# Transforms along c and back on 64x64 tiles of the array, small products on 32-column tiles, output strips queued as one step, and a new explicit order

## The chip, the cores and the metric

The kernel runs on one core of a Trainium2 chip. The metric is the device time of one execution in microseconds (us); lower is better. Five engines work side by side: PE (TensorE, matrix products and transposes, with PEld for its weight loads), DVE (VectorE), ACT (ScalarE), POOL (GpSimd) and SP, which here issues every transfer between HBM and on-chip memory. Each engine executes its own instructions in order and waits at a semaphore where it needs another engine's result.

## The reference

```python
X = np.fft.fft(x, axis=1)                 # x: 8 x 2496 x 256, f32
X = np.fft.fft(X, axis=2)
x = X.real.reshape(19968, 256)
logits = x @ phi                          # 32 slots = 8 experts x 4
d = softmax(logits, over the 19968 tokens)
slot_input = d.T @ x
for e in range(8):                        # 4 slots for each expert
    slot_out[e] = relu(slot_input[e] @ w1[e]) @ w2[e]      # 256 -> 1024 -> 256
c = softmax(logits, over the 32 slots)
return c @ slot_out                       # 19968 x 256, f32
```

The real part of the transform is never formed. The transform over the features is folded into phi, and the one over the sequence (2496 = 64 x 39) is made on the logits: first along a (64 values), then along c (39 values, of which 20 are kept by symmetry). The softmax weights over the tokens go back the same way and are multiplied with x itself.

## The kernel before

The eight batches are four pairs p = 0 to 3. The whole program is a list of steps, PLAN, written out by hand: each step calls one small function, and the order of the list is the order of the instructions on every engine. A step is a kind with its numbers, after a slash the engine of its copy (a for ACT, v for DVE, g for GpSimd), and after an equals sign the buffers in which its tiles live: `A000/a=et000:E1`. The buffers ("homes") are R (6 of 8 KB a partition: x tiles, w1, output tiles), E (18 of 4 KB: folded x, w2, turned weights), M and D (logits and exponentials), X (spread maxima) and B (the 8 banks of PSUM). A step that takes a home waits until all users of its last occupant are done; a transfer that waits for a home holds up everything behind it in SP's queue.

The kinds, in the order in which one pair goes through them:

- X, XT, C, P, I, J: loads of x (5 tiles a pair, 1024 or 896 KB), of pair 3's x once more turned over, constants, phi, w1 (8 of 1024 KB) and w2 (16 of 512 KB).
- F (or FT), G, H: folds of x on DVE, L292, L298, L303. T, A: transposes on PE (L308) and their copy. Zo, Ze, Zt, Y: products with the phi tables on 128x32 tiles (L323, L341) and copy. t, y: transpose (L362) and copy into the layout of the next step.
- a, b: transform along a (L381): for each group of three slots one product of 128 moving columns with 120 output rows. l, m: transform along c (L398), cosine and sine part, each one product of 120x120 with up to 384 moving columns. L, M, N: copy, sum and difference.
- R, V, v, vb, W, w: the maxima. E: exponentials on ACT, L448. q: sum and difference on DVE, L453.
- e, f: transform back along c (L460): for each group four products with 32 output rows, side by side on 32-column tiles, 120 moving columns each. d, D: back along a (L476). u, U: products with x (L504).
- sel, mm, mr, mx, me, ac, acT, at, si, sT: the pairs are joined and become the slot inputs (L522 to L564). This is a barrier: it needs all four pairs, and everything of the experts needs it.
- h, r, x: hidden layer (L580), relu, transpose on DVE. s, so: second layer in two halves of the output features (s0x, s1x; L598). rep, rh: each half copied to all 128 rows.
- O, Q, then ca, cb, cc, cd, ce for each half of a pair: the softmax over the slots (maximum, difference, exp, sum with reciprocal, product); lT, lc: its weights turned.
- po, ev, S: products for the output on 32x128 tiles (L681), four strips for one megabyte, their copies out of PSUM and the store. po was one step for each strip.

A float32 product appears in the trace as two matmul instructions and two weight loads, a transpose as one. No step of the output can start before s0x or s1x is complete, and the output is 20.4 MB of the 64.3 MB that the kernel moves.

Of the kernel before, what the change touches and what calls it, by code (L numbers as in the profile page):

```python
# [8 lines left out]
F32 = mybir.dt.float32  # L9
# [7 lines left out]
NPAIR = 4  # L17
# [14 lines left out]
X00=x00:R0 F00 C1 G00=e00:E0 H00 C0 P X01=x01:R1 F01 T000=bT000:B0 X02=x02:R2 T001=bT001:B1 A000/a=et000:E1  # L32
A001/a=et001:E2 G01=e01:E3 phi=bphi:B2 H01 T011=bT011:B3 F02 wphi T010=bT010:B4 A010/a H02=e02:E4 A011/a G02
T021=bT021:B5 X03=x03:R3 T020=bT020:B6 F03 H03=e03:E5 A021/a=et011:E6 G03 A020/a=et010:E7 Zo00=bz00:B7 Ze00
Y00/a=zs0:M0 T031=bT031:B0 T030=bT030:B1 A031/a t00=bt00:B2 X04=x04:R4 F04 H04=e04:E8 X11=x11:R5 Zo01=bz01:B4
T041=bT041:B3 A030/a G04 T040=bT040:B5 Ze01 y00/a=zt0:M1 A041/a=et021:E9 A040/a=et020:E10 Y01/a Zo02=bz02:B6 Ze02
Y02/a wneg F11 G11=e11:E11 H11 t01=bt01:B7 t02=bt02:B0 y01/v X10=x10:R0 F10 G10=e10:E12 T110=bT110:B1 y02/a
T111=bT111:B2 C2 a00=ba00:B3 b00/a=oo0:M2 a01=ba01:B5 b01/a a02=ba02:B4 A111/a=et101:E13 b02/a X13=x13:R1 X12=x12:R2
H10 C3 F13 H13=e13:E14 T101=bT101:B6 G13 l00=bl00:B0 A101/a m00=bm00:B7 L00/a=lt0:M3 X14=x14:R3 M00 T100=bT100:B3
A100/a=et100:E15 l01=bl01:B5 L01/a N00 m01=bm01:B2 T130=bT130:B4 F12 Zo10=bz10:B6 A110/a Ze10 A130/a=et110:E16 R00  # L40
V00=bv00:B0 T131=bT131:B3 O00=bc00:B7 H12=e12:E17 T121=bT121:B5 Y10/a=zs1:M4 G12 v00 A131/a=et111:E2 T120=bT120:B1
vb00/a=me00:X0 F14 A121/a t10=bt10:B4 A120/a W00 w00/a E001=d00:D0 E000 G14=e14:E1 M01 Zo11=bz11:B6 Ze11 H14
# [15 lines left out]
a32=ba32:B0 F31 G31=e31:E2 H31 M21 N21 R21 l20=bl20:B4 b32/a=oo3:M7 L20/a W10 w10/a m20=bm20:B7 M20 E101=d10:D1
a31=ba31:B3 b31/a V21=bv21:B6 E100 N20 R20 v21 vb21/v=me21:X1 q101=q10:D2 q100 a30=ba30:B2 b30/a O21=bc21:B0
X34=x34:R5 Q21/a=c2:M1 O11=bc11:B1 V20=bv20:B4 l31=bl31:B5 F33 L31/a=lt3:M4 E110 O22=bc22:B7 Q22/a m30=bm30:B3  # L60
l30=bl30:B2 v20 W21 vb20/a=me20:X0 L30/a w21/a m31=bm31:B0 cb00/g W20 w20/a O20=bc20:B5 e101=be101:B7 u00=bu0:B2
E210=d21:D3 E211 q111=q11:D1 q110 M31 e111=be111:B6 u01 M30 e100=be100:B4 N30 E201=d20:D0 E200 u02 f100/a=es1:M2 N31
R30 f101/a V30=bv30:B3 I1=w11:R3 X30=x30:R0 I3=w13:R4 I6=w16:R1 J13=w213:E15 J9=w29:E0 J6=w26:E3 Q11/a=c1:M6 R31
V31=bv31:B0 F30 u03 e110=be110:B4 v31 v30 Q20/a vb31/a=me31:X1 vb30/a=me30:X0 f111/a f110/a H30=e30:E4 d101=bd101:B7
d100=bd100:B1 W30 W31 sel=bsel:B5 D100/a=ds1:M3 d110=bd110:B6 D101/a q210=q21:D2 G30 q211 e210=be210:B4 w31/a w30/a
q201=q20:D1 mm G33=e33:E5 d111=bd111:B1 q200 e200=be200:B7 E300=d30:D3 e201=be201:B0 u04 H33 f210/a=es2:M7 E301
f200/a D111/a mr f201/a e211=be211:B3 ca21 E310=d31:D0 D110/v mx q301=q30:D1 u10=bu1:B5 d201=bd201:B4 q300 u11 F34
G34=e34:E8 E311 e300=be300:B7 cb21/g q311=q31:D2 D201/v=ds2:M8 f211/a q310 u12 I0=w10:R0 cc21 I2=w12:R2
d211=bd211:B6 u13 J7=w27:E12 H34 cd21 cc01 f300/a=es3:M2 cc00 e301=be301:B1 f301/a J10=w210:E11 U0/v ca20
d200=bd200:B0 D200/v cd00 e311=be311:B3 me f311/a e310=be310:B4 f310/a d210=bd210:B7 D210/a d301=bd301:B1 D211/a  # L70
cb20/v d311=bd311:B2 d300=bd300:B3 D300/a=ds3:M7 u20=bu2:B4 ac0 D311/v cd01 ce01/v d310=bd310:B0 J15=w215:E17 D301/a
J1=w21:E14 I4=w14:R5 u21 J11=w211:E13 D310/a u14 U1/v u22 u30=bu3:B7 u23 cc20 u31 u24 cd20 ac1 U2/a u32 u33 ce20/g
ce00/g u34 ac2 O12=bc12:B6 O10=bc10:B3 ac3 Q12/v acT=bac:B1 at Q10/a ca10 cb10/g ca11 O31=bc31:B2 Q31/a=c3:M2 cb11/g
O30=bc30:B0 si0=bs0:B5 O32=bc32:B4 sT0/a h010=bh01:B7 k0=bk0:B6 J3=w23:E10 J2=w22:E1 k2=bk2:B3 K2/v si1=bs1:B1 Q32/a
Q30/a ca30 lT00=bl00x:B2 J12=w212:E6 sT1/a ca31 k3=bk3:B5 cc10 J8=w28:E4 J0=w20:E16 J5=w25:E2 k1=bk1:B4 h000=bh00:B0
I5=w15:R2 K1/v K3/a I7=w17:R0 J4=w24:E9 h100=bh10:B3 h001 h110=bh11:B1 h011 K0/a tk r00=hs00:D3 cb30/v cc30
x00=hT00:E7 lc00/v=ls00:E5 s00=bo0:B5 h101 r01=hs01:D0 x01=hT01:E8 cb31/g s10=bo1:B6 cc31 s01 cd10 s11 s02 s12 cc11
s03 s13 cd11 h111 r10=hs10:D1 x10=hT10:E16 cd31 s14 r11=hs11:D2 x11=hT11:E4 s04 s15 ce21/g J14=w214:E14 s05 s16 s17
s06 so1/a rep1=br1:B4 rh1/a s07 cd30 po010=bp010:B0 po011=bp011:B2 so0/v ev011/a=o01:R5 po012=bp012:B7 ev010/v
ce11/g po013=bp013:B3 S010 rep0=br0:B1 lT02=bl02x:B6 lc02/v=ls02:E0 ev013/v lT22=bl22x:B4 lT01=bl01x:B5  # L80
lc22/a=ls22:E7 rh0/a lT12=bl12x:B2 lc12/v=ls12:E1 po041=bp041:B0 po042=bp042:B6 ev042/v=o04:R3 po043=bp043:B4
ev012/a ce10/g lc01/a=ls01:E11 S011 ev043/a po040=bp040:B1 ev041/v po022=bp022:B3 po001=bp001:B7 po003=bp003:B2
# [26 lines left out]
def _tables():  # L109
# [679 lines left out]
```

## Time and profile before

| | |
|---|---|
| median of three runs | 180.91 us (180.66 to 181.6) |
| the profiled execution | 180.69 us |
| its span, first to last instruction | 178.9 us |
| mean granted clock of PE | 0.929 of full speed |
| busy: PE, DVE, ACT, POOL | 152.6, 131.7, 102.3, 19.1 us |
| moved | 64.34 MB, 360 GB/s on average |

The span is what the trace covers; the rest of the time, 1.79 us, lies around it. A busy PE is not a PE at its peak, since matmuls are pipelined and each lasts longer than the distance to the next.

### The profile page before, as it was taken

What the parts mean: (1) busy time and instruction counts of PE and PEld (TensorE: products, weight loads), DVE (VectorE), ACT (ScalarE), POOL (GpSimd) and SP (SyncE); (2) the same over time, 40 slices, a digit from 0 to 9 for tenths busy, and PEclk for the clock granted to TensorE, in tenths of its full rate; (3) what the DMA queues carried; (4) which work ended last, traced back from release to release, by engine and by line L of the source; (5) the groups of instructions that cost most, each with busy time, mean ns of one, the idle gap of its engine ahead of it and who ended that gap; (6) DMA issues with size and microseconds to landing.
All of it is one profiled execution on the core that took longest, in us unless ns stands there. A gap on an engine that the chain in (4) does not pass through costs nothing.

```text
span 178.9 us, 5065 instructions
## 1 busy us (share of the span) xinstructions
PE 152.6 (85%) x2132; PEld 112.4 (63%) x2132; DVE 131.7 (74%) x227; ACT 102.3 (57%) x242; POOL 19.1 (11%) x22
## 2 busy tenths in 40 slices
PE   0479999999999899999989899799999997898400
PEld 0466796789787697787868774386688572444000
DVE  0589979999999998999999967865889055530600
ACT  2115748799792488999956143712895991613200
POOL 1000000000009000000200367182000000000000
PEclk9999999999999999999999999999999999655555
DMA  6999999999999999937999899840799999899994
GB/s 192 394 427 427 416 411 420 420 415 414 421 421 397 396 370 425 415 79 248 403 383 354 296 397 381 338 142 4 320 408 397 421 416 427 366 425 386 394 427 192
DMA packets 11542, 64.34 MB, mean 360 GB/s; under 512 B 1408, under 2 KB 1792, under 8 KB 6400
## 3 DMA queue, kind: packets, MB, share of 16 engines
q1 hardware_dynamic: 11520, 64.02, 90.3%
q8 instruction: 17, 0.28, 0.6%
q14 instruction: 5, 0.04, 0.1%
HBM read 43.57 MB, written 20.45 MB: 358 GB/s over the span
## 4 chain that ended last, share of the span: by engine, by line
PE 68%; DMA 14%; DVE 5%; ACT 4%; issue 2%; SPq 1%; DVEq 1%; ACTq 0%
PE B L681 12%; PE B L308 7%; DMA out<-R 7%; PE B L398 6%; PE B L381 6%; PE B L323 5%; PE B L460 5%; PE B L504 5%; PE B L476 5%; DMA R<-w1h 4%; PE B L598 4%; DMA R<-xh 4%; ACT R L230 3%; PE B L618 3%; PE B L362 3%; PE B L341 2%
## 5 line engine op out<-in xcount | busy, mean ns | idle before, releaser
L230 ACT COPY M<-B 128x320 f32<-128x320 f32 (+7 forms) x80 | 36.4, 488 | 19.4 <-PE B L323 5.2
L681 PE MATMUL B<-E,rh 32*128 32x512 f32 (+2 forms) x192 | 36.5, 621 | 2.8 <-ACT R L230 2.8
L228 DVE COPY R<-B 128x512 f32<-128x512 f32 (+1 forms) x35 | 22.2, 671 | 21.4 <-PE B L681 12.9
L230 ACT COPY R<-B 128x512 f32<-128x512 f32 (+1 forms) x45 | 23.6, 591 | 18.1 <-PE B L681 11.3
L681 PEld LDWEIGHTS B<-E,rh 32*128 32x128 f32 x192 | 21.2, 205 | 15.5 <-ACT R L230 10.8
L230 ACT COPY E<-B 128x512 f32<-128x512 f32 (+1 forms) x36 | 20.1, 582 | 15.1 <-PE B L308 13.1
L292 DVE TENSOR_TENSOR R<-R 128x1024 f32<-128x1024 f32 (+1 forms) x20 | 23.1, 1161 | 7.3 <-DMA R<-xh 7.3
L303 DVE TENSOR_TENSOR E<-R 128x512 f32<-128x512 f32 x40 | 26.0, 684 | 0.5
L308 PE MATMUL B<-cs,E 128*128 128x128 f32 x120 | 18.9, 305 | 8.5 <-DVE E L303 8.4
L308 PEld LDWEIGHTS B<-cs,E 128*128 128x128 f32 x120 | 15.6, 158 | 11.5 <-DVE E L303 9.0
L642 POOL TENSOR_TENSOR M<-M,cm 128x640 f32<-128x640 f32 x6 | 9.1, 1520 | 54.9 <-DVE cm L637 30.7
L448 ACT ACTIVATE D<-M,nm 120x128 f32<-120x128 f32 x44 | 14.0, 394 | 0.1
L460 PE MATMUL B<-cs,D 120*32 120x120 f32 x352 | 12.2, 267 | 0.8 <-issue 0.8
L323 PE MATMUL B<-E,wphi 128*32 128x256 f32 (+1 forms) x216 | 12.6, 354 | 0.0
L504 PE MATMUL B<-E,M 128*32 128x129 f32 x320 | 11.5, 274 | 0.8 <-issue 0.8
L398 PE MATMUL B<-M,cs 120*120 120x384 f32 (+1 forms) x32 | 11.6, 468 | 0.0
L658 POOL TENSOR_TENSOR M<-M,cm 128x640 f32<-128x640 f32 x7 | 9.4, 1365 | 19.6 <-DVE acc L545 13.4
L476 PE MATMUL B<-M,cs 128*32 128x320 f32 x128 | 11.2, 433 | 0.0
L460 PEld LDWEIGHTS B<-cs,D 120*32 120x32 f32 x352 | 9.7, 109 | 2.0 <-issue 1.4
L381 PE MATMUL B<-cs,M 128*120 128x128 f32 x88 | 10.8, 274 | 0.0
L504 PEld LDWEIGHTS B<-E,M 128*32 128x32 f32 x320 | 9.4, 110 | 2.2 <-issue 1.5
L381 PEld LDWEIGHTS B<-cs,M 128*120 128x120 f32 x88 | 10.3, 183 | 0.5
(92 smaller groups left out, 182.0 us busy)
## 6 DMA issues: line engine op xcount, KB each, us to landing
R<-xh SPq DMA_DIRECT2D x16, 1024.0 KB, 11.9
out<-R SPq DMA_DIRECT2D x12, 1024.0 KB, 7.2
R<-w1h SPq DMA_DIRECT2D x8, 1024.0 KB, 7.7
E<-w2h SPq DMA_DIRECT2D x16, 512.0 KB, 5.6
out<-R SPq DMA_DIRECT2D x9, 512.0 KB, 3.2
R<-xth SPq DMA_DIRECT2D x4, 1024.0 KB, 8.5
R<-xh SPq DMA_DIRECT2D x4, 896.0 KB, 11.6
out<-R SPq DMA_DIRECT2D x3, 896.0 KB, 6.3
```

The costliest lines, as they stand in the source:

```text
L228: v.tensor_copy(dst, src)
L230: sc.copy(dst, src)
L292: v.tensor_tensor(x[:, lo], x[:, lo], x[:, hi], op=ALU.add)
L303: v.tensor_tensor(d, x[:, 0:4, 0:128], x[:, 0:4, 128:256], op=ALU.subtract if k else ALU.add)
L308: pe.transpose(b[:, g * 128 : g * 128 + 128], x[:, g, k * 128 : k * 128 + 128], ident)
L323: pe.matmul(z[32 * g : 32 * g + 32, o : o + n], wphi[:, w, :], turned_x(p, u, k)[:, g].rearrange("p h q a -> p (h q a)"), start=w != 0, st ...
L381: pe.matmul(d[:120, i * 128 : i * 128 + 128], z[:, GS * g : GS * g + GS].rearrange("p s h c -> p (s h c)"), C("wa"), start=True, stop=True,)
L398: pe.matmul(b[:, : n * NA], C(("wcc", "wcs")[r]), o, start=True, stop=True)
L460: pe.matmul(b[32 * c : 32 * c + 32, o : o + 120], q[:, c // 2, i, 32 * (c % 2) : 32 * (c % 2) + 32], C(("ecc", "ecs")[c // 2]), start=True ...
L476: pe.matmul(b[32 * c : 32 * c + 32, :320], C("wb")[:, 64 * k + 32 * (c % 2) : 64 * k + 32 * (c % 2) + 32], s[:, 16 * hf : 16 * hf + 16, c ...
L504: pe.matmul(b[32 * g : 32 * g + 32, 0:129], d[:, k, c, :], x[:, c % 4, 0:129] if k == 0 else x[:, c % 4, 127:256], start=cc == 0, stop=cc ...
L681: pe.matmul(d[:, q * n : q * n + n], rh[rows, dc], l[rows, :n], start=True, stop=True, tile_position=(32 * i, 0),)
```

## The change

The groups of three slots get 64 rows for each half (60 used) in place of 120 rows in one, so that a group fills two row halves and two column halves of the array. The transform along a becomes four products a group, of 64 columns each, on two column halves. The transform along c becomes four products on the four 64x64 quarters, l and m being one step. The transform back becomes four 64x64 products a group with 60 moving columns. The products phi, sel, acT and si are cut into four 32-column tiles. The copies y and Q become two instructions where a group is not full. The four strips of po are one step. PLAN is written anew as a whole: the loads come in another order, x of pair 0 from tile 3 on, most of w1 and w2 after x; between the first load and the slot inputs no cb or ce is on GpSimd any more. DIRECT is empty, so its branch is not taken.

```diff
-HOMES = {'R': (6, 2048), 'E': (18, 1024), 'M': (10, 1408), 'D': (4, 768), 'X': (2, 120), 'B': (8, 512)}
+HOMES = {'R': (6, 2048), 'E': (18, 1024), 'M': (10, 1408), 'D': (4, 768), 'X': (2, 128), 'B': (8, 512)}
...
+DIRECT = ()
...
+X03=x03:R0 C0 F03 G03=e03:E0 T030=bT030:B0 X04=x04:R1 A030/a=et010:E1 H03 T031=bT031:B1 A031/a=et011:E2 X01=x01:R2
...
+e11=be110:B2,be111:B6 V20=bv20:B7 H31 vb21/a=me21:X1 L30/a M31 W21 M30 N31 f111/a X32=x32:R2 N30 R30 v20 R31 w21/a
+f110/a D000/a=ds0:M5 X33=x33:R0 X34=x34:R4 I1=w11:R5 d001=bd001:B4 E210=d21:D1 E211 q210=q21:D3 q211 d101=bd101:B6
...
+E200 q200=q20:D2 q201 X30=x30:R1 u11 u01 J7=w27:E15 J5=w25:E8 mm u12 J2=w22:E7 J0=w20:E5 ca11 G33=e33:E4 mr H33
...
+u34 ac1 ac2 O20=bc20:B4 ac3 acT=bac:B0 at O31=bc31:B5 si0=bs0:B3 cd00 si1=bs1:B7 k2=bk2:B1 k1=bk1:B6 cc10 sT0/a
+h100=bh10:B2 O30=bc30:B0 Q31/a=c3:M2 K2/a O32=bc32:B3 Q32/a sT1/v ce00/v lT00=bl00x:B5 lc00/a=ls00:E13 I5=w15:R4
+k3=bk3:B1 cd01 K1/v cd10 k0=bk0:B7 I6=w16:R0 h000=bh00:B3 Q20/a K3/a K0/a tk ce01/v h001 I7=w17:R3 ce10/v
+h010=bh01:B6 h011 r00=hs00:D1 h101 lT02=bl02x:B5 J9=w29:E3 x00=hT00:E14 s00=bo0:B4 s01 ca20 r01=hs01:D0 Q30/a
+J12=w212:E1 x01=hT01:E9 J8=w28:E10 h110=bh11:B1 h111 s02 s03 cb20/v lc02/a=ls02:E6 r10=hs10:D3 x10=hT10:E4 s04 s05
+J10=w210:E2 ca21 J14=w214:E5 r11=hs11:D2 J13=w213:E16 x11=hT11:E7 s06 s07 ca30 lT01=bl01x:B7 cc20 so0/a
+lc01/a=ls01:E11 rep0=br0:B3 cd11 lT10=bl10x:B6 lc10/a=ls10:E17 rh0/v po02=bp020:B0,bp021:B5,bp022:B2,bp023:B1
+po00=bp000:B4,bp001:B3,bp002:B7,bp003:B6 ca31 ev022/v=o02:R5 s10=bo1:B2 ev023/a ce11/g ev002/v=o00:R2 J15=w215:E8
+ev020/a cd20 ev021/v s11 cb31/g ev003/a po10=bp100:B1,bp101:B0,bp102:B6,bp103:B7 s12 s13 s14 S021 cc31 cd31 s15
...
         def turn_z_copy(e, p, u):
             nq = 2 if u < 2 else 1
-            d = view(f"zt{p}", GS * NG, 2, NKC)
+            z = slots(p)
...
+            copy(e, d[:, :, :, : NG - 1], b[:, :, :, :30].rearrange("p h i (g s) -> p h i g s", s=GS))
+            copy(e, d[:, :, :, NG - 1, :2], b[:, :, :, 30:])
...
             for i in range(n):
-                g = 4 * b + i
-                pe.matmul(
-                    d[:120, i * 128 : i * 128 + 128],
-                    z[:, GS * g : GS * g + GS].rearrange("p s h c -> p (s h c)"),
-                    C("wa"),
-                    start=True,
-                    stop=True,
-                )
+                for h in range(2):
+                    for r in range(2):
+                        pe.matmul(
+                            d[64 * r : 64 * r + 64, h, i], z[:, 4 * b + i, h], C("wa")[:, 64 * r : 64 * r + 64],
+                            start=True, stop=True, tile_position=(0, 64 * r),
+                        )
...
-        def along_c(p, hf, r):
+        def along_c(e, p, hf):
             g0, n = GH[hf]
-            b = view(f"b{'lm'[r]}{p}{hf}", 512, rows=120)
-            pe.matmul(b[:, : n * NA], C(("wcc", "wcs")[r]), o, start=True, stop=True)
+            for h in range(2):
+                for r in range(2):
+                    o = view(f"oo{p}", 2, NG, NA)[64 * r : 64 * r + 60, h, g0 : g0 + n].rearrange("p u k -> p (u k)")
+                    b = view(f"b{'lm'[r]}{p}{hf}", 512)
+                    pe.matmul(
+                        b[64 * h : 64 * h + 64, : n * NA], C(("wcc", "wcs")[r])[64 * r : 64 * r + 60], o,
+                        start=True, stop=True, tile_position=(64 * r, 64 * h),
+                    )
...
-            pe.transpose(b[:120, 128 : 128 + n], view(f"me{p}{hf}", GS * 40, rows=n), ident[:n, :n])
+            pe.transpose(b[:124, 128:256], view(f"me{p}{hf}", 124), ident)
...
+                    for h in range(2):
+                        rows = slice(64 * h, 64 * h + 60)
+                        b = view(f"be{p}{hf}{h}", 512)
+                        for k in range(2):
+                            tab = ("ecc", "ecn" if m else "ecs")[k]
+                            pe.matmul(
+                                b[64 * k : 64 * k + 64, 60 * i : 60 * i + 60],
+                                q[rows, i, m if direct else k], C(tab)[rows],
+                                start=m == 0, stop=m == 1 or not direct, tile_position=(64 * h, 64 * k),
+                            )
...
-            pe.matmul(b, C("ta")[:, ls], at[:, 0:32], start=True, stop=False)
-            pe.matmul(b, C("tb")[:, ls], at[:, 32:64], start=False, stop=True)
+            for m, tab in enumerate(("ta", "tb")):
+                for g in range(4):
+                    pe.matmul(
+                        b[32 * g : 32 * g + 32],
+                        C(tab)[:, lc * 128 + 32 * g : lc * 128 + 32 * g + 32],
+                        at[:, 32 * m : 32 * m + 32],
+                        start=m == 0, stop=m == 1, tile_position=(0, 32 * g),
+                    )
...
-        def product(e, p, b, i):
+        def product(e, p, b):
+            l = view(f"ls{p}{b // 2}", 512 if b < 4 else 256)
+            for q, dc in enumerate(strip(b, 0)[1]):
+                for i in range(4):
...
+            gp.memset(mneg, 0.0)
+            for i in range(HOMES["X"][0]):
+                gp.memset(home[f"X{i}"], 0.0)
```

Counted in the two lists, the steps ahead of the copy sT0 differ in these: cd 4 before and 1 after, ca 6 and 4, cb on GpSimd 5 and 0 and on DVE 1 and 4, ce on GpSimd 2 and 0 and on DVE 1 and 0, D on DVE 4 and 1, Y and y on DVE 3 and 1, O 12 and 10, I 6 and 5, J 8 and 9, si 1 and 2, k 0 and 2. All other kinds stand there in the same number, but for e (one step takes the place of two) and l with m. Each group of e has as many matmul instructions as before, each group of a four times as many.

## Rows read from the trace of the kernel before

**Rows 1.** The page: busy time of the engines, and DMA rate in 40 slices.
```profile
PE 152.6 (85%) x2132; PEld 112.4 (63%) x2132; DVE 131.7 (74%) x227; ACT 102.3 (57%) x242; POOL 19.1 (11%) x22
...
GB/s 192 394 427 427 416 411 420 420 415 414 421 421 397 396 370 425 415 79 248 403 383 354 296 397 381 338 142 4 320 408 397 421 416 427 366 425 386 394 427 192
```

**Rows 2.** Windows: busy us (instructions) of each engine, clock, DMA share, GB/s.
```profile
0.00:5.40 5.40, 0.00 (x0) 0.00 (x0) 0.01 (x1) 1.28 (x1) 0.46 (x7) 1.00 0.66 217
...
5.40:105.70 100.30, 94.99 (x1538) 76.62 (x1539) 94.69 (x159) 67.64 (x173) 7.99 (x8) 1.00 0.96 380
105.70:125.30 19.60, 18.46 (x381) 11.54 (x381) 13.13 (x31) 7.76 (x17) 10.63 (x8) 1.00 0.63 232
125.30:178.90 53.60, 39.19 (x217) 24.22 (x215) 23.91 (x39) 25.59 (x51) 0.00 (x0) 0.76 0.93 382
```

**Rows 3.** The chain that ended last: shares of the span by line.
```profile
by line: PE B L681 12.2%; PE B L308 7.1%; DMA out<-R 6.6%; PE B L398 5.6%; PE B L381 5.5%; PE B L323 5.5%; PE B L460 5.4%; PE B L504 5.2%; PE B L476 4.9%; DMA R<-w1h 4.0%; PE B L598 3.7%; DMA R<-xh 3.7%; ACT R L230 3.0%; PE B L618 2.8%; PE 
```

**Rows 4.** The chain in order of time: start, us, what; 107 to 119 us.
```profile
107.15 7.21 DMA R<-w1h
...
114.41 1.06 PE B L580 x8
115.47 3.06 PE B L598 x112
```

**Rows 5.** The same chain where PE changes its tile shape, 33 to 57 us.
```profile
33.11 0.88 PE B L308 x8
...
36.00 1.02 PE B L308 x8
...
53.44 1.00 PE B L323 x16
...
56.28 0.86 PE B L323 x16
```

**Rows 6.** Groups by line and shape: busy us, mean ns, idle before.
```profile
L681 PE MATMUL B<-E,rh 32*128 32x512 f32 x128 | 34.5, 747 | 2.8 <-ACT R L230 2.8
...
L460 PE MATMUL B<-cs,D 120*32 120x120 f32 x352 | 12.2, 267 | 0.8 <-issue 0.8
...
L228 DVE COPY M<-B 128x320 f32<-128x320 f32 x5 | 2.4, 480 | 0.1
...
L228 DVE COPY M<-B 128x512 f32<-128x512 f32 x2 | 1.4, 682 | 1.0 <-PE B L362 1.0
...
L230 ACT COPY sT<-B 128x32 f32<-128x32 f32 x2 | 0.4, 186 | 1.0 <-PE B L561 1.0
```

**Rows 7.** Timeline of PE: 16 products of one column each.
```profile
108.15 0.31 PE L490 MATMUL B<-cs,M 128*32 128x1 f32 x16
```

**Rows 8.** Timeline of DVE, 92 to 97 us: cd, then cb.
```profile
92.54 0.81 DVE L651 TENSOR_REDUCE cm<-M 128x20 f32<-128x640 f32 x1
...
93.79 0.23 DVE L228 COPY usb<-B 128x129 f32<-128x129 f32 x1
...
96.30 0.76 DVE L642 TENSOR_TENSOR M<-M,cm 128x640 f32<-128x640 f32 x1
96.98 0.28 DVE L542 TENSOR_SCALAR acc<-usb,sm 128x129 f32<-128x129 f32 x1
```

**Rows 9.** Single lines: duration in ns, shortest, median and longest.
```profile
L298 DVE TENSOR_TENSOR R<-R x5: 1160/1214/2281, 51.6 to 59.7; 128x1024 f32<-128x1024 f32 x4, 128x768 f32<-128x768 f32 x1
...
L545 DVE SCALAR_TENSOR_TENSOR acc<-usb,sm,acc x2: 256/782/1308, 101.1 to 101.5; 128x129 f32<-128x129 f32 x2
```

**Rows 10.** Timeline of POOL: GpSimd's early steps, 53 to 104 us.
```profile
53.74 2.11 POOL L642 TENSOR_TENSOR M<-M,cm 128x640 f32<-128x640 f32 x1 [23.29 <-ACT E L230]
...
101.38 2.54 POOL L658 TENSOR_TENSOR M<-M,cm 128x640 f32<-128x640 f32 x2 [13.37 <-DVE acc L545]
```

**Rows 11.** Timeline of SP: the last load of x, the last two of w1.
```profile
62.06 0.33 SPq L242 DMA_DIRECT2D R<-xh  x1
...
107.15 2.58 SPq L252 DMA_DIRECT2D R<-w1h  x2
```

More of the change, by code (lines that the diff above doesn't have):

```diff
@@ L33 @@
[L33 to L42, printed above, removed]
@@ L58 @@
[L58 to L67, printed above, removed]
@@ L68 @@
[L68 to L82, printed above, removed]
@@ L129, in block, with halves @@
         return np.kron(eye, t)
+    def halves(t, cols):
+        a = np.zeros((128, cols))
+        a[:60, : t.shape[1]] = a[64:124, : t.shape[1]] = t
+        return a
     half = np.where(kc == 0, 0.5, 1.0)[:, None]
@@ L146, in _tables @@
         [
-            ("ecc", block(half * np.cos(ga).T)),
-            ("ecs", block(np.sin(ga).T)),
+            ("ecc", halves(block(half * np.cos(ga).T), 60)),
+            ("ecs", halves(block(np.sin(ga).T), 60)),
+            ("ecn", halves(block(-np.sin(ga).T), 60)),
             ("onehot", onehot),
@@ L265, in phi_tables @@
                     tab = C(name)[:, lc * 128 : lc * 128 + 128]
-                    pe.matmul(b[:, i * 32 : i * 32 + 32], tab, phi[:, lc, :], start=lc == 0, stop=lc == 1)
+                    for g in range(4):
+                        rows = slice(32 * g, 32 * g + 32)
+                        pe.matmul(
+                            b[rows, i * 32 : i * 32 + 32], tab[:, rows], phi[:, lc, :],
+                            start=lc == 0, stop=lc == 1, tile_position=(0, 32 * g),
+                        )
             for lc in range(2):
@@ L521, in pair_max @@
                 n = GH[hf][1]
-                pe.matmul(
-                    b[:, : NPAIR * GS], C("sel")[:n, 128 * hf : 128 * hf + 128],
-                    mneg[:n, hf].rearrange("p a s -> p (a s)"), start=hf == 0, stop=hf == 1,
-                )
+                for g in range(4):
+                    pe.matmul(
+                        b[32 * g : 32 * g + 32, : NPAIR * GS],
+                        C("sel")[:, 128 * hf + 32 * g : 128 * hf + 32 * g + 32],
+                        mneg[:, hf].rearrange("p a s -> p (a s)"),
+                        start=hf == 0, stop=hf == 1, tile_position=(0, 32 * g),
+                    )
         def pair_max_mask(e):
@@ L548, in gather_turn @@
             b = view("bac", 512)
-            pe.matmul(b[:, 0:64], acc[:, 1:129], C("psum"), start=True, stop=True)
+            for g in range(4):
+                pe.matmul(
+                    b[32 * g : 32 * g + 32, 0:64], acc[:, 1 + 32 * g : 33 + 32 * g], C("psum"),
+                    start=True, stop=True, tile_position=(0, 32 * g),
+                )
             pe.matmul(b[:1, 64:96], acc[:, 0:1], C("psum")[:, 0:32], start=True, stop=True)
```

212 lines of the change are left out of this document (110 added, 102 removed).

## The prediction

> **What bounds the kernel now.** I read the page first, then the windows by stage, the chain, and the groups by line. The page gives no engine as the plain bound: PE 85% busy, DVE 74%, and a transfer rate with holes in it, above all the slices at 79, 142 and 4 GB/s [rows 1]. The windows divide the span at three events: the first fold (5.40), the slot inputs (copy sT0, 105.7) and the first store (125.3).
>
> From 5.4 to 105.7 us PE is busy 94.99 and DVE 94.69 of 100.3 us, DMA 96% [rows 2]. Three resources are nearly full together, ACT has room with 67.64. Which of the two engines sets the pace can't be read from one number, so I price the change on both and let the one with less relief decide. From 105.7 to 125.3 the experts' layers run; DMA falls to 63% [rows 2], and the chain shows why the stage is long: 7.21 us of it are a w1 load [rows 4]. From 125.3 on there are 53.6 us of stores at 382 GB/s, with PE, DVE and ACT far from full [rows 2]. That stage is as long as its bytes, so the end follows the first store.
>
> **The change, first stage (up to sT0).** Terms on PE:
>
> l and m: the chain gives L398 5.6% of 178.9, or 10.0 us [rows 3]. Four quarters at once take half the passes: 5.0, a saving of 5.0. The trace shows four column tiles going together (352 instructions of 267 ns at L460 in 12.2 us) and four row tiles (128 of 747 ns at L681 in 34.5) [rows 6], never both at once; so the bounds are 20 us (four quarters one after the other) and 5.0. I take 5.0, since each kind alone overlaps fully.
>
> e: L460 is 5.4%, 9.7 us for 352 matmul instructions, in 88 passes of four at 110 ns [rows 3, 6]. The instructions stay 352, the moving columns fall from 120 to 60, so the stream halves to 4.85. The other bound is the rate at which instructions start: 16 products of one column end within 0.31 us of the first start [rows 7], at most 19 ns each, and taking off the length of the last less. At 19 ns, 352 would need 6.7 us, and nothing would be saved only above 27 ns. I take 4.85, saving 4.85; the range keeps 0.
>
> The Trainium skill has a rule against this part: "TensorEngine Tiling (Array Packing)", section Instruction Overhead, says that a product costs about 60 cycles however few columns it has. If that were paid one product after another, an estimate by its figure is 352 x 60 / 2.4 GHz = 8.8 us, and e would save 0.9. The 16 products above stand against paying it in series.
>
> a: the instructions go from 88 to 352 and the columns of each from 128 to 64, two side by side. L381's 5.5% [rows 3], 9.8 us, stays: 352 in 9.8 us is 28 ns each, slower than the 19 of [rows 7]. Zero; if half the overlap of the two column halves failed, +4.9.
>
> The small products: sel, acT and si are a few instructions each; four narrow weight loads together in place of a wide one save about 0.5 us. phi lies under the first loads.
>
> Changes of tile shape: the trace prices one. The same eight transposes take 0.88 us behind work of the same shape and 1.02 behind narrow tiles, the same 16 phi products 0.86 and 1.00 [rows 5]: 0.14 us at each change. The list changes shape 23 times ahead of sT0 before and 47 times after: 24 x 0.14 = +3.4 us.
>
> The Trainium skill says in "TensorEngine Tiling (Array Packing)", section Key Properties, that changing the tiling mode drains the engine. Taken as a full drain, an estimate is the 267 ns that an L460 product lasts less the 110 ns between passes, 0.157 us, and the term would be 3.8; the 0.14 of the row agrees.
>
> PE: -5.0 - 4.85 - 0.5 + 3.4 = -7.0 us, leaving 88.0.
>
> Terms on DVE, from the counts of steps in the two lists. Three cd leave the stage: one occupies DVE from 92.54 to 93.79, 1.25 us [rows 8], so -3.75. Two ca leave it, a reduce of the same 640 values as cd's first, 0.81 [rows 8]: -1.6. Three cb come and one ce goes, at 0.68 from start to start [rows 8]: +1.4. Three D go to ACT at 0.48, and two full Y or y at 0.68 [rows 6]: -1.4 each. Together -6.75.
>
> GpSimd: while it works at 53.7 and at 101.4 [rows 10], one FT lasts 2.28 where the median is 1.21, and one ac 1.31 where the other took 0.26 [rows 9]. I put these 2.1 us down to sharing memory with GpSimd; with no cb or ce on it in this stage they go. Bounds 0 and 2.1; I take 2.1. DVE: -6.75 - 2.1 = -8.9, leaving 85.8.
>
> ACT gains the second copies: 12 for y and 3 for Q of some 0.19 us [rows 6], 2.8; three D, less than the 0.48 each that they cost on DVE, 1.4; Y and y, 1.2; less one Q of about 0.6. +4.8 leaves 72.4, still under 73% of the stage if this becomes about 93 us. Nothing else gains.
>
> PE is now the fuller again. At the share of today (94.99 of 100.3, 0.947) 88.0 us of work take 92.9, and sT0 stands 7.4 earlier, at 98.3. With DVE's relief alone (85.8 at 0.944) it would be 9.4 earlier. The start moves little: the first fold needs a tile of 1024 in place of 896 KB, 131,000 bytes at 217 GB/s [rows 2] is 0.6 us, against a constant table of 256 KB that no longer shares this time.
>
> **Second stage.** Before, w15 goes where w12 lay (R2), so its load waits for h010, is issued at 107.15 with w17's [rows 11], lands 7.21 us later, and only then come the two last h with all that follows, 10.9 us to the first store [rows 4]. Now I5 takes R4 from x tile 34 and needs no h. I6 waits for h100, I7 for h000, which stands some 3.5 us behind sT0 (one h, two O, one lT). With 7.2 us to land again, h111 runs 10.7 behind sT0. Then follow relu and transpose (1.4), s06 and s07 (0.9; at the chain's 3.06 us for 112 instructions [rows 4] one s step takes 0.44), so0, rep0, rh0 (1.2), po02 and two copies (2.3): 5.8. That gives 16.5, less if the load lands sooner. PE's own work in that stretch is eight h of 0.9 (1.06 with a change of shape [rows 4]), eight s of 0.44, four lT, two O, rep and po02, about 14 us, and with six changes of shape and the waits at the relus 17. I take 17.5, 2.1 less than the 19.6 now; the bounds are 16.5 and 19.6. The first store needs s0x alone; s1x and J15 come behind it.
>
> **Third stage.** Same bytes, same banks, same copies, with po's strips merely queued together: PE is idle for 14 of the 53.6 us there, which hides it. GpSimd's eight remaining steps lie beside stores. J15 (0.52 MB) now falls into the stage, +1.3 us. 54.9 us.
>
> Sum: 98.3 + 17.5 + 54.9 = 170.7 us of span. The profiled execution is 1.79 longer than its span, and within 0.3 of the median: **172.5 us**. Check by bytes: 43.9 MB of loads at the 415 of full slices [rows 1] fit ahead of the first store at 115.8.
>
> **Rivals.**
>
> Small products no shorter: e stays at 9.7 us because its instructions, not its columns, set the pace. PE's relief is 2.1, sT0 2.2 earlier, the time 177.7. For it speaks that 60 columns are few; against it [rows 7]. It is the way of the rule on instruction overhead that the Trainium skill gives in "TensorEngine Tiling (Array Packing)". Chance 0.10.
>
> ACT's longer queue: each copy on ACT now stands behind more work ahead of PE's next product, and if PE waits out ACT's extra 4.8 us, less what it idles today anyway, sT0 is only some 3 earlier: 177. For it: ACT grows while the others shrink. Against it: it is busy for only three quarters of the stage. Chance 0.11.
>
> All of DVE's relief arrives and stores run at 415 GB/s: 95.8 + 16.5 + 50.5, a time of 164.6 to 168. For it: DMA waits less for freed buffers. Chance 0.10.
>
> Slower: SP's queue. X30 takes R1 from x tile 31 and is behind H31 (fold of pair 3) in time; before, the last x load went out at 62.06 [rows 11]. Behind X30 stand 14 J, six I: with itself 14.7 MB, then 20.45 MB of output. At 415 GB/s that is 84.7 us, and 3 to land. If X30 goes out later than 91 us, the end is later than now, whatever the engines do; each further us costs one. By the rows' durations some 61 of DVE's 85.8 us stand ahead of H31, which at today's share is 70 us into the span; so it takes 20 us of slip, from loads or from DVE's order. Chance 0.10, and 0.07 that a smaller loss on this road just eats the gain.
>
> Quarters one after the other: l is 20 us in place of 5, PE's work 103, sT0 8.5 later than now, about 188. Against it: both single overlaps in [rows 6]. Chance 0.03.
>
> **How the numbers follow.** The likeliest case, 0.49, gives 172.5, with 168 to 176.5 as its own range. A measurement of this kernel tells about 0.5% (0.9 us) from no change. Faster: 0.49 + 0.10 + 0.11 + 0.10 = 0.80; same 0.07; slower 0.13. The range from 165 to 180 leaves out the slower cases and a little at the low end.
>
> **What would show it.** L460's share and L398's at half of 5.4 and 5.6%; windows up to sT0 with PE near 88 us; sT0 near 98; first store near 116; no wait of 7 us for w1 in the chain; FT never 2.28. Wrong if L460 keeps its time, if a DMA gap before sT0 exceeds 8 us, or if the store stage is longer than 56 us.

## The result and the profile after

The changed kernel takes 182.9 us (median of 4 runs, 182.64 to 183.53) against 181.06 for the kernel before beside it (180.66 to 181.6): a ratio of 1.0105, interval 1.0064 to 1.0145. It is about 1% slower. The forecast was 172.5 us, its range ended at 180: direction and size are both wrong.

The windows of the changed kernel, cut at the same three events (first fold, copy into sT, first store); columns as in [rows 2]:

```profile
0.00:5.40 5.40, 0.00 (x0) 0.00 (x0) 0.00 (x0) 1.28 (x1) 1.01 (x12) 1.00 0.67 229
5.40:111.90 106.50, 92.06 (x1909) 69.67 (x1911) 85.62 (x143) 74.01 (x191) 0.48 (x4) 0.97 0.87 345
111.90:128.20 16.30, 16.22 (x275) 8.96 (x262) 14.49 (x33) 8.54 (x21) 2.27 (x2) 1.00 0.84 330
128.20:181.40 53.20, 35.32 (x336) 21.00 (x332) 26.87 (x47) 28.10 (x56) 7.67 (x7) 0.79 0.96 393
```

The second stage takes 16.3 us (19.6 in [rows 2], 17.5 forecast), the third 53.2 (53.6, 54.9 forecast). Everything was lost in the first: the copy into sT is at 111.9 where 98.3 was forecast and 105.7 stood before. DVE there is busy 85.62 us, as forecast (85.8). PE is at 92.06, not 88.0, and it stands still for 14 us where 5 stood before.

Where it stands still is in its waits, summed by line (total us, times, longest):

```profile
PE B L318 <- DVE E L313: 9.0, 3, 7.8
PE B L480 <- issue: 7.3, 3, 3.8
...
PE B L394 <- issue: 1.4, 1, 1.4
PE B L394 <- ACT M L235: 0.8, 2, 0.4
PE B L522 <- issue: 0.7, 1, 0.7
PE B L372 <- ACT M L235: 0.6, 2, 0.4
```

L480 is the back transform e, L394 is a, L522 the inputs products u. "issue" is a wait for nothing that the profile knows: no semaphore, no buffer. It takes 9.4 us; before it was 1.6 (0.8 of it at L460 in [rows 6]). The chain has it as 6.4% of the span, beside ACT's copies into M (4.6%; the y copies are among them). It shows l and m halved as forecast (L398 5.6% in [rows 3], L410 2.9% here); e fell too, but not to half (L460 5.4%, L480 3.7%):

```profile
by line: PE B L711 10.1%; PE B L318 6.9%; PE B L494 6.4%; issue 6.4%; PE B L394 6.2%; DMA out<-R 5.6%; PE B L333 5.6%; PE B L522 5.2%; ACT M L235 4.6%; PE B L628 4.1%; PE B L610 4.0%; DMA R<-xh 3.7%; PE B L480 3.7%; PE B L410 2.9%; PE B L69
```

PE's timeline shows what is odd about these stops: they fall inside a step, among instructions of one kind, and the profile shows no input that is waited for.

```profile
64.09 2.79 PE L394 MATMUL B<-cs,M 128*64 128x64 f32 x88 [0.44 <-ACT M L235]
66.81 1.50 PE L480 MATMUL B<-cs,D 60*64 60x60 f32 x85
71.16 0.27 PE L480 MATMUL B<-cs,D 60*64 60x60 f32 x2 [2.85 <-issue]
...
86.24 2.83 PE L522 MATMUL B<-E,M 128*32 128x129 f32 x96
89.00 1.51 PE L480 MATMUL B<-cs,D 60*64 60x60 f32 x88
90.43 0.41 PE L522 MATMUL B<-E,M 128*32 128x129 f32 x3
91.50 1.52 PE L522 MATMUL B<-E,M 128*32 128x129 f32 x45 [0.66 <-issue]
92.95 1.49 PE L480 MATMUL B<-cs,D 60*64 60x60 f32 x83
98.23 0.48 PE L480 MATMUL B<-cs,D 60*64 60x60 f32 x5 [3.80 <-issue]
98.64 7.13 PE L494 MATMUL B<-M,cs 128*32 128x320 f32 x64
```

The first of these e steps runs its 88 records in 1.5 us, where 88 took 2.4 before (a quarter of the 9.7 us of L460). The second runs 83 records, then nothing for 3.8 us, then the other five. (A product in the code is two matmul and two weight-load instructions in the trace; records are counted here.) The page offers one thing that could be late: queue 8, "instruction". It carried 17 packets in the kernel before and these here (packets, MB, share):

```profile
q8 instruction: 19, 0.31, 0.7%
```

19 packets of 16 KB; PE has 2 x 2494 instructions, which is 19.5 times 256. The kernel before has 2 x 2132, 16.7 times 256.

Behind the longest stop come two more losses. The granted clock over 98.7 to 105.6 us is 0.62 of full, a mix of the two levels 1.2 and 2.4 GHz, and the 64 records of d take 7.1 us at it instead of 4.5 (as in e13, below). DVE waits 5.46 us for the pairs' exponentials (L559), which ACT forms behind its copies of these e and d steps.

### The profile page after: what moved, and what is told of

Read it like the earlier page. It is cut to its first block, busy times and chain, and to the rows that moved or that the text cites. A ratio compares the mean times of both kernels' runs of the same rounds, so it can differ in the third digit from the quotient of the medians.

```text
span 181.4 us, 5827 instructions
## 1 busy us (share of the span) xinstructions
PE 143.6 (79%) x2494; PEld 99.6 (55%) x2494; DVE 127.0 (70%) x222; ACT 111.9 (62%) x268; POOL 11.4 (6%) x24
## 4 chain that ended last, share of the span: by engine, by line
PE 65%; DMA 9%; ACT 7%; issue 6%; DVE 4%; SPq 0%; ACTq 0%; DVEq 0%
PE B L711 10%; PE B L318 7%; PE B L494 6%; PE B L394 6%; DMA out<-R 6%; PE B L333 6%; PE B L522 5%; ACT M L235 5%; PE B L628 4%; PE B L610 4%; DMA R<-xh 4%; PE B L480 4%; PE B L410 3%; PE B L693 3%; PE B L648 2%
## 5 line engine op out<-in xcount | busy, mean ns | idle before, releaser
L235 ACT COPY M<-B 128x480 f32<-128x480 f32 (+11 forms) x101 | 44.2, 524 | 17.5 <-PE B L480 6.0
L235 ACT COPY R<-B 128x512 f32<-128x512 f32 (+1 forms) x49 | 25.3, 592 | 12.0 <-PE B L711 6.6
L711 PE MATMUL B<-E,rh 32*128 32x512 f32 (+2 forms) x192 | 29.8, 589 | 2.8 <-ACT R L235 1.6
L235 ACT COPY E<-B 128x512 f32<-128x512 f32 (+1 forms) x37 | 21.1, 583 | 16.4 <-PE B L318 15.1
L318 PEld LDWEIGHTS B<-cs,E 128*128 128x128 f32 x120 | 15.9, 162 | 12.2 <-DVE E L313 10.2
L463 ACT ACTIVATE D<-M,nm 124x128 f32<-124x128 f32 x44 | 14.2, 400 | 0.0
L480 PE MATMUL B<-cs,D 60*64 60x60 f32 x352 | 7.4, 222 | 7.3 <-issue 7.3
L394 PE MATMUL B<-cs,M 128*64 128x64 f32 x352 | 11.4, 223 | 2.2 <-issue 1.4
L428 DVE TENSOR_TENSOR M<-M,B 124x320 f32<-124x320 f32 (+1 forms) x16 | 8.0, 513 | 7.0 <-ACT M L235 6.9
L394 PEld LDWEIGHTS B<-cs,M 128*64 128x64 f32 x352 | 10.8, 138 | 4.0 <-issue 4.0
L687 POOL TENSOR_TENSOR M<-M,cm 128x640 f32<-128x640 f32 x5 | 6.3, 1264 | 86.7 <-DVE cm L682 86.7
L480 PEld LDWEIGHTS B<-cs,D 60*64 60x64 f32 x352 | 6.5, 135 | 8.5 <-issue 8.2
L522 PE MATMUL B<-E,M 128*32 128x129 f32 x320 | 9.9, 274 | 0.7 <-issue 0.7
L522 PEld LDWEIGHTS B<-E,M 128*32 128x32 f32 x320 | 8.8, 110 | 1.4 <-issue 0.9
L468 DVE TENSOR_TENSOR D<-D 124x320 f32<-124x320 f32 (+1 forms) x16 | 7.8, 512 | 1.8 <-ACT D L463 1.8
```

Source lines behind the costliest of these rows:

```text
L235: sc.copy(dst, src)
L318: pe.transpose(b[:, g * 128 : g * 128 + 128], x[:, g, k * 128 : k * 128 + 128], ident)
L394: pe.matmul(d[64 * r : 64 * r + 64, h, i], z[:, 4 * b + i, h], C("wa")[:, 64 * r : 64 * r + 64], start=True, stop=True, tile_position=(0, ...
L463: sc.activation(d[:, g], L[:, g], AF.Exp, bias=nms[:, p, hf, g : g + 1], scale=1.0)
L480: pe.matmul(b[64 * k : 64 * k + 64, 60 * i : 60 * i + 60], q[rows, i, m if direct else k], C(tab)[rows], start=m == 0, stop=m == 1 or not ...
L522: pe.matmul(b[32 * g : 32 * g + 32, 0:129], d[:, k, c, :], x[:, c % 4, 0:129] if k == 0 else x[:, c % 4, 127:256], start=cc == 0, stop=cc ...
```

## The experiments

The code in this section is shortened. Theory "supply": PE gets its instructions in blocks of 256, one per some 5.6 us while transfers run, and a stretch that uses them faster stops. Rivals: ACT's y copies (L235, 128x480, the 8 of y 1.27 us each, where y took 0.59 before) set the pace; or the products' time alone ("sum"), the stops being time that PE would have waited anyway. In the first expectations the theories also go by letters: the one on the y copies is A, the one that counts PE's instructions is C; D and E hold that waits for other engines, or the work itself, set the time.

**e1: y copies that write runs of c.** Only the order of the copy's loops.

```
-d = z[..., :60].rearrange("p g h (s c) -> p h c g s", s=GS)[:, :, 8*u : 8*u + 4*nq]
+d = z[..., :60].rearrange("p g h (s c) -> p g s h c", s=GS)[..., 8*u : 8*u + 4*nq]
```

> Only the order of the elements inside the two copies y changes: eight neighbouring values along c are written in a row, as before the change, where the changed kernel writes single values 20 apart. Theory A (the scattered write is what makes y last 1.27 us in place of 0.59 on ACT, and ACT is on the chain at 36 to 42 and 58 to 64 us): y back to about 0.6, ACT's busy time 6 to 8 us less, sT0 from 112 to 103 to 107, time 174 to 179. Theory B (two instructions in place of one, or four dimensions in the pattern, cost it, not the order of writing): y stays above 1.1 us and the time at 182 to 184. Theory C (PE's supply of instructions is the bound, ACT only follows): y gets short and the time stays at 181 to 184.

181.33 us, ratio to before 0.9991 (0.9957 to 1.0024). The 16 copies of 480 columns (8 for y, 8 for Q) fall from the first row, of the changed kernel, to the second, of e1:

```profile
L235 ACT COPY M<-B 128x480 f32<-128x480 f32 x16 | 14.1, 916 | 0.7 <-PE B L372 0.7
```

```profile
L235 ACT COPY M<-B 128x480 f32<-128x480 f32 x16 | 9.0, 566 | 0.8 <-PE B L372 0.8
```

So scattered writes cost 0.7 us a copy, and the kernel 1%. PE's waits for ACT's copies into M (1.4 us in the list above) are gone; its issue stops stayed at 8.8 us. The copies got short and the time lies at C's 181 to 184; A's 174 to 179 us failed.

**e2, e3: back transform on four 128x32 tiles, as before, without and with e1's copies.** As many records as the 64x64 form (352), twice the columns.

> Undoes one part: the transform back along c goes on 32-column tiles again, 120 moving columns for a group, with the same 352 matmul instructions; plan and all else stay as changed. PE's own work for it rises by 3 to 5 us. Theory C (PE runs e faster than its instructions arrive, and stops for 2.85 us at 68 and 3.8 us at 94 in the middle of a step until the next ones are there): the stops shrink to under 1.5 us each, the granted clock stays at 1.00 up to sT0, and the time is 178 to 182 in spite of the added work. Theory D (the stops are waits for other engines in the new order): the stops stay, PE's work is longer, time 184 to 188.

> Both edits at once: y written in runs and the transform back on 32-column tiles. If A and C are both right and independent, the gains add: 170 to 177, sT0 at 98 to 104. If the two losses lie side by side (each hidden behind the other), the gain is about that of the better one alone.

183.25 us (1.0107, 1.0013 to 1.0201) and 181.87 (1.0011, 0.9953 to 1.007). Both forecasts of the supply theory failed: in e2 the stops were to shrink under 1.5 us each (the longest is 2.9) and the time to 178 to 182, in e3 to 170 to 177. The quarters are no culprit by themselves; with the same number of instructions the stops stay (8.1 us in e2). In e2 the clock held at 1.00 over the d steps (4.3 us for 64 records), and its profiled execution still has the copy into sT at 110.5, 4.7 behind the kernel before. So the low clock costs what d lost, but is not the cause by itself.

**e4: the supply by itself.** Ahead of everything, 1536 products on 64x64 quarters from one constant, with no input to wait for.

```
+for i in range(384):
+    for h in range(2):
+        for k in range(2):
+            pe.matmul(bank[h][64*k : 64*k+64, :60], ident[64*h : 64*h+60, :64],
+                      ident[64*h : 64*h+60, :60], tile_position=(64*h, 64*k))
```

> Measures the disputed cost by itself: ahead of the first fold, 1536 products on 64x64 quarters with 60 columns (3072 matmul instructions and as many weight loads), all from one constant table, so that none waits for another engine; transfers of x run beside them for the first 17 us and then stop, since all buffers are full. Theory C: PE works in bursts of 256 instructions with stops between them, above 1 us long while transfers run; when they have stopped, the stops shorten. All 384 groups take well over 41 us. Theory D: no stops, 107 to 120 ns for each group of four products, 41 to 46 us in all, then the kernel as it is.

269.4 us, 86 more than the changed kernel. PE's timeline:

```profile
6.08 6.19 PE L408 MATMUL B<-cs 60*64 60x60 f32 x223 [6.08 <-DMA cs<-c]
14.67 3.02 PE L408 MATMUL B<-cs 60*64 60x60 f32 x128 [2.40 <-issue]
21.14 3.68 PE L408 MATMUL B<-cs 60*64 60x60 f32 x128 [3.44 <-issue]
...
43.78 2.09 PE L408 MATMUL B<-cs 60*64 60x60 f32 x128 [1.37 <-issue]
47.51 2.09 PE L408 MATMUL B<-cs 60*64 60x60 f32 x128 [1.64 <-issue]
51.52 2.09 PE L408 MATMUL B<-cs 60*64 60x60 f32 x128 [1.92 <-issue]
```

128 records with their 128 loads, 256 instructions, then a stop, again and again. The burst takes 2.09 us (8 ns an instruction), its period is 3.5 to 4.0 us while the transfers rest (5 GB/s from 36 to 90 us) and 6.5 us while x still loads (14.67 to 21.14). Queue 8 has 43 packets, 24 more, and the 6144 added instructions are 24 times 256. The stop is the supply of instructions, as theory C had it. That 446 go before the first stop is why a short row of products shows nothing of it. The trace also has the time of each packet: all 22 stops of this row end 1.2 to 1.6 us behind the end of a packet of queue 8.

With that the five issue stops of the changed kernel can be told apart. Four end 1.2 to 1.5 us behind the end of a packet, and PE ran 127, 382 and 128 records from each to the next: one block, three, and one. The longest, from 94.44 to 98.23, has one packet in it (95.74 to 96.75; the row is queue 8 in the window 94.4 to 98.3):

```profile
q8 instruction: 1, 0.02, 1.6%
```

The fifth is another thing. The 1.40 us ahead of the first a end at 26.68, 5.4 us behind the last packet, but just when ACT's first y copies end (23.12 + 3.52 = 26.64). In e1 these copies end at 24.34, a starts at 24.35, and the stop is gone. The first two rows are of the changed kernel, the last of e1:

```profile
26.68 2.79 PE L394 MATMUL B<-cs,M 128*64 128x64 f32 x88 [1.40 <-issue]
23.12 3.52 ACT L235 COPY M<-B 128x512 f32<-128x512 f32 x7 [0.37 <-PE B L333]
```

```profile
22.24 2.10 ACT L235 COPY M<-B 128x512 f32<-128x512 f32 x7 [0.37 <-PE B L333]
```

So of the 9.4 us, 8.0 are the supply and 1.4 a wait for ACT that the profile does not name; e2 and e5, which keep the scattered copies, have this stop too.

**e5: a and c whole in the changed kernel**, 296 records fewer:

```
-    d[64*r : 64*r+64, h, i], z[:, 4*b+i, h], C("wa")[:, 64*r : 64*r+64], tile_position=(0, 64*r),
+    d[:, i*128 : i*128+128], z[:, 4*b+i].rearrange("p h q -> p (h q)"), C("wa"),
-    b[64*h : 64*h+64, :n*NA], C(("wcc","wcs")[r])[64*r : 64*r+60], o, tile_position=(64*r, 64*h),
+    b[:, :n*NA], C(("wcc","wcs")[r]), o,
```

**e6: that, with e1's copies, whole small products and e as two products on 128x64 tiles.** 1956 records in all. **e7: that e in the kernel before.** **e9: e7 with d on 64-column tiles.** The e of e6 and e7, as the edit of e7 against the kernel before:

```
-for c in range(4):  b[32*c : 32*c+32, o : o+120], q[:, i, c//2, 32*(c%2) : 32*(c%2)+32], C(("ecc","ecs")[c//2])
+for k in range(2):  b[64*k : 64*k+64, o : o+120], q[:, i, k], C(("ecc","ecs")[k])
```

> The changed kernel with the transforms along a and c taken back from the tiles: one full product a group along a (88 matmul instructions in all in place of 352), two full ones along c (32 in place of 64), same 64-row halves, same plan, 64x64 back transform kept. PE's streaming work rises by some 5 us, its instructions up to the slot inputs fall by 296 matmuls and as many weight loads, 592, that is 2.3 blocks of 256. Theory C (up to sT0 PE gets no more than one block in 5.5 to 6.5 us while transfers run, so the count of instructions sets the stage): sT0 8 to 13 us earlier than 112, time 171 to 177. Theory E (work on the engines and the order set the stage, the stops only fill gaps that would be there anyway): 182 to 187.

> The same with y written in runs, the small products whole again, and the back transform as two products a group on 128x64 tiles (176 matmul instructions in place of 352, 120 columns each, streaming time as before the change). Against the changed kernel 538 matmuls and as many loads fewer, 4.2 blocks of 256; streaming work up by about 10 us. Theory C: sT0 at 92 to 100, time 165 to 173. Theory E: 180 to 188, since PE streams 10 us more.

> The kernel before, one edit: the back transform along c as two products a group on 128x64 tiles in place of four on 128x32, same columns, same outputs; 176 matmul instructions and 176 loads fewer, 1.4 blocks. Streaming time is the same. Theory C holds for the kernel before as well (between 72 and 105.7 us it ran 746 matmuls and as many loads in 33.7 us, 5.8 us for 256): sT0 4 to 8 us earlier, time 173 to 177. Theory E: 180 to 182, nothing changes but the count.

> As the last one, and back along a as two products on 128x64 tiles in place of four on 128x32 (64 matmul instructions in place of 128). In all 240 matmuls and 240 loads fewer than before, 1.9 blocks. Theory C: one to three us faster than the last one, 170 to 176. Theory E: 180 to 182.

Medians beside 181.39 for the kernel before (178.44 to 182.92, too wide for a verdict on differences of 1 or 2%): e5 184.02, e6 179.27, e7 181.52, e9 183.73. The forecasts of the supply theory failed in all four (171 to 177, 165 to 173, 173 to 177, 170 to 176); theory E was right on e5 and e7 and missed e6 and e9. The sums show why: they priced the instructions and forgot the products. PE's time up to the copy into sT, added up from the timeline, from the start of each group to that of the next less the idle time shown (us):

```
                   before  after    e5     e6     e7     e8    e11    e12    e13
a                    9.8   11.0   10.3   10.2    9.8   10.2   10.2   11.2   11.4
l and m             10.2    5.4   10.1   10.1   10.2   10.1   10.1    5.3    5.5
e                    9.8    6.9    6.0    9.8   11.1    6.7    8.2    8.0    9.8
d                    8.6   11.5    9.2    8.9    9.4   10.2    8.9    8.9    8.9
all other steps     56.9   57.8   57.0   60.0   57.7   59.4   59.4   59.1   55.9
sum                 95.4   92.6   92.6   98.9   98.2   96.6   96.8   92.5   91.5
stops on "issue"     1.6    9.4    5.7    0.7    0.9    4.3    0.3    4.4    1.8
other idle           1.9    2.6    3.4    1.2    1.2    1.2    1.6    1.2    1.2
copy into sT at    105.8  111.9  109.6  108.6  107.2  109.6  106.2  105.9  102.3
```

The rows add up to the last one within 0.5 us with the first product, at 7.1 to 8.0 us. Before, there were only 1.6 us of stops to win, so e7 wins 0.7 and pays 1.3 in the time of e. In e5 the stops fall by 3.7, but whole l and m cost 4.7. e6 has 0.7 us of stops left and pays for it with 6.3 us of products more than the changed kernel. Products and supply have to be weighed stretch by stretch. The next forecasts were made from its first five columns.

**e8**: e6 with e on 64x64 quarters. **e11**: e8 with e on 128x64 tiles for the last two pairs alone, which stand among the inputs products. **e12**: e11 with a and c on quarters again.

> The changed kernel with y copies that write runs of c, with a and c as whole 128-row products and the small products whole; the back transform stays on four 64x64 tiles. Added up by TensorE's steps up to the first copy into sT: 92.6 us in the changed kernel, less 2.8 that its d steps lost at the lower clock, plus 4.0 for whole a and c, plus 1.9 for whole small products: 95.6, behind a start at 7.8 and 1.2 of waits on DVE, with 71.7 us from that copy to the end. Theory 'supply' (TensorE gets 256 instructions per some 5.7 us, and stops where a stretch holds more): the stretch of inputs and back transforms at 85 to 98 us keeps nearly all its 350 products, so 3 to 4.5 us of stops and perhaps the lower clock stay: about 181 us (180 to 183). Rival 'sum' (stops are not what sets the end, only the products' time is): 176 us.

> The kernel of e8 with the back transforms of the last two batches, which stand among the inputs products, as two products on 128x64 tiles: 88 fewer products of the 350 in that stretch, each step 1.0 us longer. Theory 'supply': the stops in that stretch go (under 1 us left), 1.95 us of products are added: the copy into sT at about 107, 179 us (178 to 180), faster than e8 although its products take longer. Rival 'sum': 178 us, 2 us slower than e8.

> The kernel of e11 with a and c back on four 64x64 tiles: 296 more products, 4 us less of their time. Theory 'supply': stops of 3.4 to 4.5 us come at 64 to 78 us, where the products of z turned, a, e and c stand together, and take the 4 us back: 179 us (177.5 to 180.5). Rival 'sum': 174 us.

e8 182.04 us, ratio 1.0073 (1.0022 to 1.0125); e11 178.68, 0.9856 (0.9782 to 0.9929); e12 179.28, 0.9919 (0.9888 to 0.9949). The supply theory gave 181, 179 and 179; the rival had e8 faster than e11, and e12 at 174. The same stretch in e8, and then in e11:

```profile
87.73 1.51 PE L469 MATMUL B<-cs,D 60*64 60x60 f32 x88
89.17 1.53 PE L511 MATMUL B<-E,M 128*32 128x129 f32 x48
90.63 0.68 PE L469 MATMUL B<-cs,D 60*64 60x60 f32 x31
94.41 1.41 PE L469 MATMUL B<-cs,D 60*64 60x60 f32 x57 [3.10 <-issue]
```

```profile
88.82 2.48 PE L473 MATMUL B<-cs,D 124*64 124x120 f32 x44
91.23 1.53 PE L529 MATMUL B<-E,M 128*32 128x129 f32 x48
92.68 2.48 PE L473 MATMUL B<-cs,D 124*64 124x120 f32 x44
95.09 3.17 PE L501 MATMUL B<-M,cs 128*32 128x320 f32 x44
```

The two slower steps (2.48 us each instead of 1.4 to 1.5) take 1 us longer each than the fast ones; a stop of 3.1 and one of 1.2 behind it are gone.

**e13: the changed kernel with e1's copies and the 128x64 e of e6 for all pairs.** a, c and the small products stay as the change has them. It differs from e3 only in two tiles of 64 columns instead of four of 32.

> The kernel of e3 (y copies in runs of c, back transform on 32-column tiles, everything else as in the changed kernel) with that back transform as two products on 128x64 tiles in place of four on 128x32: 176 instead of 352 products, each twice as long, the same copies and buffers. Theory 'supply': the stops at the back transforms among the inputs products go (4.3 us in e2) and most of those at 66 to 68 us, while an early one of 1.4 us stays: products 92.5, waits on DVE 1.2, stops 2.5, start 7.8: the copy into sT at 104, then 71 us of span and 1.8 around it: 177 us (175.5 to 179). Rival 'sum': the same exchange in the kernel before added 1.3 us to the back transform and changed no time (e7), so here 182 to 183 us, as in e3 or above it.

175.87 us, ratio to before 0.9765 (0.9695 to 0.9835): faster than the kernel before by 1.7 to 3.1%, and below the changed kernel's 182.9. Forecast: 177 by supply, 182 to 183 by the sum. The early stop of 1.4 us that the forecast kept is gone: it was the y copies'. The stretch that lost most in the changed kernel reads, in e13:

```profile
83.54 2.48 PE L481 MATMUL B<-cs,D 124*64 124x120 f32 x44
85.95 1.53 PE L523 MATMUL B<-E,M 128*32 128x129 f32 x48
87.40 2.48 PE L481 MATMUL B<-cs,D 124*64 124x120 f32 x44
89.81 4.51 PE L495 MATMUL B<-M,cs 128*32 128x320 f32 x64
94.14 3.24 PE L523 MATMUL B<-E,M 128*32 128x129 f32 x106
98.83 1.74 PE L523 MATMUL B<-E,M 128*32 128x129 f32 x54 [1.45 <-issue]
```

and its first stage ends 9.6 us earlier than the changed kernel's, with the transfers busy again (0.95 against 0.87) and the clock at 1.00:

```profile
5.40:102.30 96.90, 91.37 (x1731) 70.70 (x1735) 85.50 (x143) 69.12 (x191) 0.48 (x4) 1.00 0.95 379
```

The list of steps is the changed kernel's, word for word. So neither that order nor SP's queue made the kernel slower.

## Why the prediction was wrong

**l and m: right.** -5.0 forecast, -4.8 measured (10.2 to 5.4 in the table).

**e: this step failed.** It took the stream as halved to 4.85 us and named as the other bound "the rate at which instructions start", at most 19 ns from 16 products [rows 7]. The records did run at 16 ns instead of 27, so four steps without a stop would take 5.7 to 6 us; the table has 6.9, a saving of 2.9. But the rate at which instructions start is not the rate at which they come, and for that the sum had no term: 8.0 us of stops, 7.3 of them in e, so that e with its stops took 14.2 us where 10.6 stood. Sixteen products are 32 instructions, and e4 ran 446 before its first stop. From 85.65 to 98.64 us the changed kernel has 352 records, 704 instructions or 2.75 blocks. From one stop's end to the next one's, 71.16 to 77.47 and 91.50 to 98.23, a block took 6.3 and 6.7 us; at that pace 2.75 blocks are 17 to 18 us, and the products themselves take 8.5. The kernel before was near this limit already: it has two stops of 0.8 us in the middle of steps, 255 records or two blocks apart, each ending 1.2 to 1.3 us behind a packet's end. One of them is the "issue 0.8" of L460 in [rows 6], and I did not ask what they were. In the changed kernel queue 8 has 9 packets from 62 to 112 us, one per 5.6 us on average, a gap in the transfers included:

```profile
q8 instruction: 9, 0.15, 1.2%
```

The Trainium skill says in "Runtime: NRT & Kernel Launch", section Instruction fetch mechanics, that an engine's instructions are streamed in 16 KiB blocks of 256 and that crossing a block's boundary is mostly hidden. The packets and the bursts of 128 records with their loads agree with the blocks. Most of the 19 blocks here pass without a stop, but the 8.0 us at four of them and the 1.4 to 1.9 at each block in e4 do not agree with "mostly hidden".

**a: half wrong.** Zero was forecast; its products cost 1.2 more. The stop of 1.4 in front of the first is ACT's (above). Its 264 more records also use up a block each 128, which the step did not price.

**Small products:** -0.5 forecast, -1.9 measured; phi alone -1.3, which was taken to lie under the first loads. **Changes of shape:** +3.4 forecast; the steps that no edit touched grew by 2.7 (turning x 2.0, turning z 0.4, z 0.2). In e13, with the same list and nearly the same shapes, the same three are only 0.9 longer than before, which leaves about that at most for the changes of shape; the cause of the rest wasn't isolated.

**Not foreseen:** d, +2.9 at the lower clock behind the longest stop. All in all PE's products came to -2.8 instead of -7.0, idle time to +8.5 instead of less, the start to +0.6 (named in the prediction, but left out of its sum): 6.1 us later instead of 7.4 earlier.

**DVE, GpSimd: right.** 85.62 us against 85.8; no fold of the turned x above 1.23 us (2.28 in [rows 9]). The relief bought nothing because PE was the later one. **ACT:** +6.4 against +4.8; the y copies' scattered writes were not priced, and cost 1% (e1): PE waited 1.4 us for them at 26.68 and 1.4 in other places. Two figures in the prediction are slips without effect on its sum: 72.4 us are 78% of 93, not under 73%, and with DVE's relief of 9.4 the copy into sT would stand at 96.3, not 95.8.

**Second and third stage: right** within 1.2 and 1.7 us; the 7 us wait for w1 is gone from the chain.

Of the rivals, "small products no shorter" came nearest, by the wrong road: the products were shorter (16 ns a record), and what set the pace was instructions per stretch of time, not cycles per instruction. "ACT's longer queue" was a small part. "SP's queue" was not it: the gap in the transfers before sT is there (X30 is issued at 78.2 and J7 waits to 86.4), beyond the 8 us named as a sign, but no product waited for it, and e13 has the same queue.

**Open:** why a block takes 5.9 to 6.8 us beside transfers (between neighbouring stops of e1, e2, e4, e5 and the changed kernel) and 3.5 to 4.0 without; why the clock fell behind this stop, and in e8 behind one of 3.1 us, and not behind e2's of 2.9 or the changed kernel's own of 2.85; what the new tile forms give in the order of before, which wasn't tried.

## What to carry to other kernels

Beside the time of each product on PE, count the instructions of each stretch, weight loads included: here PE was given 38 to 43 per us between stops while transfers ran, and a row of 64x64 quarters of 60 columns uses 122. Where a stretch asks for more than it gets, a form with fewer and longer products wins even though its own time is longer (e13 against e1, which differ in e alone: e +3.4 us, stops -6.9, and d, l and m -3.8, since the clock now stays at 1.00). Where there are few stops there is nothing to win (e7). A wait on "issue" in the middle of a step, however short, can mean that this limit is near: look whether a packet of the instruction queue landed just before its end, and whether the stops lie whole blocks apart. The 1.4 us ahead of a were "issue" as well and had another cause.

## What was not expected of the hardware

PE stopped after each 256 instructions for 1.4 to 1.9 us with no other engine busy, when they lasted 2.09 us (e4), and each of these stops ended 1.2 to 1.6 us behind the end of a packet of queue 8. A copy of 480 columns by ACT took 0.7 us longer when it wrote single elements apart than when it wrote runs (0.92 us mean of 16 against 0.57, half of them unchanged; e1). The granted clock was 0.62 over the 7 us behind a stop of PE of 3.8 us, and 1.00 in e13, where no stop was longer than 1.45.
